# Moving the weight operations of a second MLP between the stages of a fused kernel

## The chip, the cores and the metric

The kernel runs on one core of one Trainium2 chip. The time is device microseconds from launch to end, the median of three runs. Five engines work beside each other, each through its own instructions in order: TensorE (PE in the profile, its weight loads PEld), VectorE (DVE), ScalarE (ACT), GpSimd (POOL) and SyncE (SP), which here issues nearly all DMA transfers. They wait for each other through semaphores.

## The reference

Attention without a softmax feeds two MLPs, all in float32:

```
kv  = einsum('bhsd,bhse->bhde', k, v)          # 8 batches, 8 heads, 576 rows, 64 columns
out = einsum('bhsd,bhde->bhse', q, kv)
x   = out / sqrt(mean(out*out, -1) + 1e-6) * g_norm      # then laid out as 4608 x 512
h   = x @ w_in                                 # 512 x 2048
y   = (s * max(h, 0)**2 + b) @ w_out           # 2048 x 512
z   = max(max(y @ w1, y @ w2), y @ w3)         # each 512 x 768
res = z @ w_out2                               # 768 x 512
```

## The kernel before, in words

A float32 product is made of three fast products. Each operand is split into a high part (ScalarE, a copy to the `float32r` type) and a low part (VectorE, the difference); high by high, low by high and high by low are summed in PSUM. The 4608 rows of x are nine tiles of 512. The weights come as 64-bit words and are converted on the core.

The stages, in order of time:

- **Opening and plain tiles** (tiles 0 and 1, first MLP): the start follows a list written out by hand (`OPENING`), the rest the loop over `slots` behind it. A slot is one block of 128 columns of h (there are 16, taken in groups of 3, 5 and 8): twelve up products `h`, the squared ReLU, its split (`gh`, `gl`: the gate), and twelve down products `y` two slots later. The last group of tile 1 is in this loop with `fa` = 8.
- **Tile 2** (`EDGE - 1`): the loop over `f` does the 16 up products and stores the squared ReLUs to `g_dr`, except for the last two blocks, which are gated directly. Then the pools of the plain stage close, and the class `Second` does the 16 down blocks: first the two direct ones, then blocks 0 to 13, whose squared ReLUs are loaded again as `gb` (`fetch`) and gated (`ready`).
- **Pairs 0, 1 and 2** (tiles 3 and 4, 5 and 6, 7 and 8): up products of two tiles at once by a seven-product scheme, by eight chunks `q` of two blocks each (products named `x`, `d`, `a`, `b`; ScalarE copies `a`, `p7`, `u2` between them), then a second half by `Second` for the second tile of the pair.
- **Second MLP**, from about 830 us on, with the same scheme for w1, w2, w3 and w_out2.

Attention for the tiles still to come runs beside all this in small steps (`rare_steps`): an item is `ops` (its products), `sq`, `og`, `sh`, `sl`, then `mps` (a mean by products with ones), `y`, `t` and the result `og`; `kvps` and `kvbd` make the matrix of a pair of heads.

The second MLP needs its weights combined for the seven-product scheme: nine operations `com_op(0)` to `com_op(8)` and three `out_op`. Each is made by `fused` (line 598 on): a load of two raw tiles, then for each of them `high` (ScalarE, L194) and `rest` (VectorE, L199 to L209), `sums` (VectorE, four differences, L696), `to_hi` (four copies on ScalarE, L639), `to_lo` (four on VectorE, L644) and six stores to `wc_dr`. Before, operations 0 and 1 stand beside tile 2's up products, 2 and 3 beside the second half of pair 0, 4 to 7 beside pair 1, and 8 in the second MLP.

What sets the order: `beside_of(fns, a, b)` spreads a list of steps evenly over a range of the clock `tick` counts (one tick for each TensorE product; `ONE` is 12). `store` puts a transfer off by some ticks, `dma` issues it at its place in the program. `tied_in` keeps a step behind the main work already written on ScalarE and VectorE (`in_order`). Within these ties a scheduler places each instruction on its engine when the program is built; what it decided is what `order` rows below show.

Memory: `rawp`, `wtp`, `wt1` and `stp` (raw tiles, two tables, staging tiles) belong to the plain stage; the pools of the pairs take the same memory when it closes. From then on the attention items share one PSUM bank (`ps_as`) where they had two.

Of the kernel before, what the change touches and what calls it, by code (L numbers as in the profile page):

```python
# [71 lines left out]
def fused_kernel(ctx, tc, qt, kv, kvr, g_norm, w_in, w_out, s, b, w1, w2, w3, w_out2, out):  # L72
# [525 lines left out]
    def fused(srcs, turned, target, dst, raws=None, tabs=wide, his=hi_tile):  # L598
# [42 lines left out]
        def to_lo(*ks):  # L641
            for k in ks:
                hi, lo, src = pieces()[k]
                nc.vector.tensor_tensor(out=lo, in0=src, in1=hi.bitcast(F32), op=ALU.subtract)  # L644

        def end():
            if target:
                if dst is not None:
                    store(dst, got["to"].bitcast(F32))
                return  # L650
            raw = blocks(got[0])
            to = [(0, 0, 2, got["to"].bitcast(F32)), (0, 2, 3, raw[:, 0:1]), (1, 0, 3, raw[:, 1:4]), (0, 3, 7, blocks(got[1]))]
            to += [(1, o, o + 2, blocks(t)) for o, t in zip((3, 5), got["tab"])]
            for z, a, e, t in to:
                store(dst[:, z, a:e], t, 12)

        def last():
            to_lo(*range(4))
            end()

        fns = [partial(high, 0), partial(rest, 0), none, partial(high, 1), partial(rest, 1), sums, none]
        if target:
            def both(k):
                to_hi(k + 1)
                to_lo(k)

            def close():
                to_lo(2)
                end()

            return load, fns + [partial(to_hi, 0), partial(both, 0), partial(both, 1), close]
        return load, fns + [partial(to_hi, *range(4)), last]

# [7 lines left out]

    def phased(op, before, behind):
        load, fns = op
        return [load] + [none] * before + [partial(tied_in, fn) for fn in fns] + [none] * behind

# [783 lines left out]
    pend = [(*slots[k], gates[k][1:]) for k in range(OPEN) if f"yy.{k}.0" not in ran]  # L1469

    todo, span, k_done, base = [], 1, 0, 0
    for i, sl in list(enumerate(slots))[OPEN:]:
# [10 lines left out]
        for half in range(2):  # L1483
            if half:
                if len(pend) == LAG:
                    u2(*pend.pop(0))
                pend.append((*sl, u1_end(h, n)))
            want = min(len(todo), -(-len(todo) * (2 * i + half + 1 - base) // span))
            while k_done < want:
                todo[k_done]()  # L1490
                k_done += 1


# [22 lines left out]

    def com_op(i, here=False, **homes):
        def target():
            wm[i] = wc_tile("wb" if i % 3 == 2 else "wa")
            return wm[i]  # L1520

        (ja, ma), (jb, mb) = sides_of(i)
        ws = w1, w2, w3
        return fused([chunk(ws[jb], mb), chunk(ws[ja], ma)], False, target if here else None, wc_dr[i], **homes)

    ONE = 3 * KD
# [4 lines left out]
    with in_order():  # L1531
        roots()
    beside_of(rare_steps(*groups[4]), 0, 24 * ONE)
    homes = {
        "raws": lambda: rawp.tile([P, 2 * DM], U32, tag="raw", name="raw"),
        "tabs": lambda: [p_.tile([P, DM], U32, tag=tg, name="tab") for p_, tg in ((wt1, "ta"), (wtp, "tb"))],
        "his": lambda: stage().bitcast(F32R).rearrange("p (n c) -> p n c", c=HW),
    }
    seq = []
    for i in range(2):  # L1540
        load, (h0, r0, _, h1, r1, sm, _, hi, lo) = com_op(i, **homes)
        seq += [load, none] if i == 0 else [none, load]
        seq += [lambda h0=h0, r0=r0: tied_in(h0, r0), lambda h1=h1, r1=r1: tied_in(h1, r1)]
        seq += [partial(tied_in, sm), partial(tied_in, hi), partial(tied_in, lo)]
    beside_of(seq, 2 * ONE, 16 * ONE)
    for f in range(KF):
        h = u1(t, 0, TW, f)
        if pend:
            u2(*pend.pop(0))
        r = wtp.tile([P, DM], U32, tag="tb", name="r").bitcast(F32) if f < 3 else stage()  # L1550
        squared(r, h)
        if f < KF - 2:
            store(g_dr[t][f], r)
        else:
            direct[f] = gate(r)
        tick(ONE)

# [256 lines left out]
    for s, (ta, tb) in enumerate(PAIRS):  # L1814
# [4 lines left out]
        if s == 1:  # L1819
            ops = [com_op(i) for i in range(4, NQ - 1)] + [out_op(KC - 1)]  # L1820
            beside_of([fn for op in ops for fn in phased(op, 4, 4)], 0, V + U - 12)
        if s == 2:
# [6 lines left out]
        for q in range(QF):  # L1829
            w = wcs.pop(q)  # L1830
            if s == 0 and 0 < q and q + 1 < QF:
                beside_of([prep.step], 3, 10)
            if s > 0 and 0 < q and q + 1 < QF:
                wcs[q + 1] = pair_load("wa", wp_dr[q + 1])
# [48 lines left out]
        beside_of(nxt, 10, 5 * QF * 6 - 8 if blk else U - 24)  # L1883
        if s == 0:
            beside_of([fn for i in (2, 3) for fn in phased(com_op(i), 3, 3)], 0, U - 12)
        if s + 1 < len(PAIRS):
# [24 lines left out]
    ops = [out_op(0, True), out_op(1, True), com_op(NQ - 1, True)]  # L1911
    inside += [fn for op in ops for fn in phased(op, 3, 1)]
    for si in range(len(SUPERS)):
# [100 lines left out]
```

## Time and profile before

| | |
|---|---|
| median of 3 runs | 1392.78 us (1390.97 to 1395.8) |
| profiled execution, its own time | 1389.79 us |
| span of the profile, first to last instruction | 1387.8 us |
| TensorE busy | 1361.1 us, 98% |
| VectorE busy | 994.7 us, 72% |
| ScalarE busy | 777.4 us, 56% |
| mean granted clock of TensorE | 0.996 |
| moved by DMA | 311.42 MB |

The time to read is the profiled execution's 1389.79, of which the span leaves 2 us outside. TensorE's busy time counts a product from its start to its modelled end, and neighbours overlap; a stretch where it is busy all the time can still be slow if its clock is low. A wait in square brackets at the end of a timeline row is the idle time of the engine ahead of that row, with the instruction that ended it.

### The profile page before, as it was taken

How to read it: one execution, taken by the hardware profiler on the slowest of the kernel's cores; microseconds unless marked ns; L12 is line 12 of the kernel's file. 1: busy time of each engine (PE TensorE's matmuls, PEld its weight loads, DVE VectorE, ACT ScalarE, POOL GpSimd, SP SyncE). 2: the span in 40 equal slices, each digit the busy share in tenths (PEclk: the TensorE clock that was granted, in tenths of full speed). 3: DMA queues.
4: the chain of work that ended last, by engine and by line, in shares of the span. 5: the costliest groups of instructions: out<-in, count | busy, mean ns of one | idle time of the engine just before them, and what ended most of it. 6: DMA issues, size and time to landing. Idle time of an engine off the chain costs nothing.

```text
span 1387.8 us, 19621 instructions
## 1 busy us (share of the span) xinstructions
PE 1361.1 (98%) x6822; PEld 1123.2 (81%) x6822; DVE 994.7 (72%) x1896; ACT 777.4 (56%) x1520; POOL 10.9 (1%) x40
## 2 busy tenths in 40 slices
PE   8999999989999999999999999999999999999998
PEld 6878787867888877888788878888998888888886
DVE  8998866868767578768667786797683675666555
ACT  7975655646777557667456775444453442444332
POOL 1000000000000000000000000000000000000000
PEclk9999999989999999999999999999999999999999
DMA  8486643778576686886847889656865554563432
GB/s 305 145 255 207 206 151 131 239 241 288 204 262 213 198 329 225 303 306 224 326 146 287 284 298 329 241 182 258 302 242 177 186 209 152 178 254 111 173 149 61
DMA packets 140457, 311.42 MB, mean 224 GB/s; under 512 B 50118, under 2 KB 71750, under 8 KB 131398
## 3 DMA queue, kind: packets, MB, share of 16 engines
q1 hardware_dynamic: 140352, 310.17, 64.2%
q8 instruction: 54, 0.88, 0.3%
q14 instruction: 45, 0.37, 0.1%
q10 hardware_dynamic: 6, 0.00, 0.0%
HBM read 218.89 MB, written 91.23 MB: 223 GB/s over the span
## 4 chain that ended last, share of the span: by engine, by line
PE 79%; DVE 10%; ACT 4%; DMA 4%; issue 2%; SPq 0%; DVEq 0%; ACTq 0%
PE x L520 19%; PE y L520 16%; PE d L520 12%; PE o L520 9%; PE b L520 6%; PE a L520 6%; PE h L445 3%; PE h L155 2%; PE y L155 2%; DVE tb L155 1%; PE ops L365 1%; DMA raw<-in_w_out 1%; DMA wq<-wo_dr 1%; PE kvps L343 1%; DMA wc<-ws_dr 1%
## 5 line engine op out<-in xcount | busy, mean ns | idle before, releaser
L520 PE MATMUL y<-gh,w 128*128 128x512 f32 x720 | 238.3, 394 | 2.2 <-ACT st L544 1.4
L520 PE MATMUL d<-t,wc 128*128 128x512 f32 (+1 forms) x828 | 200.0, 376 | 1.3 <-ACT p L810 1.3
L520 PE MATMUL x<-t,wc 128*128 128x512 f32 (+1 forms) x828 | 200.0, 376 | 0.0
L520 PEld LDWEIGHTS d<-t,wc 128*128 128x128 f32 x828 | 148.5, 188 | 29.5 <-ACT p L810 1.7
L520 PEld LDWEIGHTS x<-t,wc 128*128 128x128 f32 x828 | 148.4, 188 | 27.8 <-DVE t L181 0.2
L520 PEld LDWEIGHTS y<-gh,w 128*128 128x128 f32 x720 | 135.9, 189 | 30.6 <-ACT st L544 1.8
L520 PE MATMUL y<-gl,w 128*128 128x512 f32 x360 | 142.5, 396 | 1.7 <-DVE gl L503 1.6
L874 DVE TENSOR_TENSOR c<-d,u 128x512 f32<-128x512 f32 (+1 forms) x45 | 28.7, 638 | 115.6 <-PE d L520 115.5
L520 PE MATMUL a<-b,wc 128*128 128x512 f32 (+1 forms) x414 | 100.3, 376 | 0.0
L520 PE MATMUL x<-b,wc 128*128 128x512 f32 (+1 forms) x414 | 100.0, 376 | 0.0
L520 PE MATMUL b<-b,wc 128*128 128x512 f32 (+1 forms) x414 | 99.9, 377 | 0.0
L520 PEld LDWEIGHTS b<-b,wc 128*128 128x128 f32 x414 | 73.9, 188 | 15.3 <-ACT b L810 1.8
L520 PEld LDWEIGHTS x<-b,wc 128*128 128x128 f32 x414 | 74.3, 188 | 13.9 <-DVE c L878 0.2
L520 PEld LDWEIGHTS a<-b,wc 128*128 128x128 f32 x414 | 74.2, 188 | 13.9
L520 PEld LDWEIGHTS y<-gl,w 128*128 128x128 f32 x360 | 68.2, 189 | 17.1 <-DVE gl L503 4.1
L520 PE MATMUL o<-t,wq 128*128 128x512 f32 (+1 forms) x354 | 75.5, 369 | 0.0
L155 PE MATMUL h<-xh,w 128*128 128x512 f32 (+1 forms) x216 | 72.0, 377 | 0.7 <-ACT r L155 0.6
L869 ACT ACTIVATE a<-x 128x512 f32<-128x512 f32 (+1 forms) x45 | 24.3, 539 | 86.1 <-PE x L520 86.1
L520 PEld LDWEIGHTS o<-t,wq 128*128 128x128 f32 x354 | 62.4, 188 | 11.2
L503 DVE SCALAR_TENSOR_TENSOR gl<-r,cst,gh 128x512 fp32r<-128x512 f32 x56 | 42.0, 749 | 40.6 <-ACT gh L502 40.1
L869 ACT ACTIVATE b<-x 128x512 f32<-128x512 f32 (+1 forms) x45 | 24.3, 539 | 77.5 <-PE x L520 77.4
L155 PE MATMUL y<-gh,w 128*128 128x512 f32 (+1 forms) x200 | 65.3, 371 | 0.9 <-ACT st L155 0.9
(241 smaller groups left out, 2673.6 us busy)
## 6 DMA issues: line engine op xcount, KB each, us to landing
wc<-wc_dr SPq DMA_DIRECT2D x44, 1792.0 KB, 7.5
wc<-wp_dr SPq DMA_DIRECT2D x16, 1792.0 KB, 8.8
kv<-in_kv SPq DMA_DIRECT2D x32, 512.0 KB, 4.9
wp_dr<-wc SPq DMA_DIRECT2D x8, 1792.0 KB, 6.7
raw<-in_w_out SPq DMA_DIRECT2D x23, 512.0 KB, 5.0
gb<-g_dr SPq DMA_DIRECT2D x46, 256.0 KB, 5.5
g_dr<-r SPq DMA_DIRECT2D x43, 256.0 KB, 2.3
y_dr<-st SPq DMA_DIRECT2D x42, 256.0 KB, 3.0
```

Source lines behind the costliest of these rows:

```text
L155: tail[eng] = call(*args, **kw).ins
L343: nc.tensor.matmul(pb[d, i * D:(i + 1) * D], lhsT=t[:, 0, d], rhs=t[:, 1, d], start=(c == 0), stop=(c == NC))
L365: nc.tensor.matmul(pb, lhsT=l, rhs=r, start=(i == 0), stop=(i == 2))
L445: nc.tensor.matmul(h[:, :n], lhsT=w[:, z, kk, :], rhs=x[:, kk, o:o + n], start=(i == 0), stop=(i == 3 * KD - 1))
L503: nc.vector.scalar_tensor_tensor(out=gl, in0=r, scalar=b, in1=gh.bitcast(F32), op0=ALU.add, op1=ALU.subtract).ins,
L520: ins = nc.tensor.matmul(*args, **kw)
L869: main["act"] = nc.scalar.activation(out=out, in_=pb, func=ACTF.Copy).ins
L874: main["dve"] = nc.vector.tensor_tensor(out=o, in0=pb, in1=t, op=ALU.add).ins
```

## The change

`fused` issues its stores at their place (`dma`) and returns one plain list of steps, the stores being a step of their own; `phased` takes a string that says, for each step of the spread, what is done: `L` load, `h` and `r` the two conversion steps, `s` the sums, `a` and `b` the high and low parts, `e` the stores, a dot nothing. Operation 0 goes into the last group of tile 1, one step each half slot. Operations 1 and 2 go beside tile 2 from its first tick over 150 ticks (before: operations 0 and 1 from tick 24 to 192), with the clock counted in two halves of a block. Operation 3 begins in chunk 7 of pair 0 and runs 153 ticks on, into that pair's second half, where 2 and 3 were. Both tables of the early operations now come from `wt1`. The strings for pair 1 and the second MLP keep the same steps with the stores as a step behind.

```diff
--- before.py
+++ after.py
@@ -646,30 +646,24 @@
         def end():
             if target:
                 if dst is not None:
-                    store(dst, got["to"].bitcast(F32))
+                    dma(out=dst, in_=got["to"].bitcast(F32))
                 return
             raw = blocks(got[0])
             to = [(0, 0, 2, got["to"].bitcast(F32)), (0, 2, 3, raw[:, 0:1]), (1, 0, 3, raw[:, 1:4]), (0, 3, 7, blocks(got[1]))]
             to += [(1, o, o + 2, blocks(t)) for o, t in zip((3, 5), got["tab"])]
             for z, a, e, t in to:
-                store(dst[:, z, a:e], t, 12)
-
-        def last():
-            to_lo(*range(4))
-            end()
-
-        fns = [partial(high, 0), partial(rest, 0), none, partial(high, 1), partial(rest, 1), sums, none]
+                dma(out=dst[:, z, a:e], in_=t)
+
+        fns = [partial(high, 0), partial(rest, 0), partial(high, 1), partial(rest, 1), sums]
         if target:
             def both(k):
                 to_hi(k + 1)
                 to_lo(k)
 
-            def close():
-                to_lo(2)
-                end()
-
-            return load, fns + [partial(to_hi, 0), partial(both, 0), partial(both, 1), close]
-        return load, fns + [partial(to_hi, *range(4)), last]
+            fns += [partial(to_hi, 0), partial(both, 0), partial(both, 1), partial(to_lo, 2), end]
+        else:
+            fns += [partial(to_hi, *range(4)), partial(to_lo, *range(4)), end]
+        return load, fns
 
     def tied_in(*fns):
         with in_order():
@@ -679,9 +673,10 @@
     def none():
         pass
 
-    def phased(op, before, behind):
+    def phased(op, order):
         load, fns = op
-        return [load] + [none] * before + [partial(tied_in, fn) for fn in fns] + [none] * behind
+        fns = [partial(tied_in, fn) for fn in fns]
+        return [load if c == "L" else none if c == "." else fns.pop(0) for c in order]
 
     def sides_of(i):
 
@@ -1468,6 +1463,21 @@
     OPEN = next(k for k in range(len(slots)) if f"up.{k}.0" not in ran)
     pend = [(*slots[k], gates[k][1:]) for k in range(OPEN) if f"yy.{k}.0" not in ran]
 
+    def com_op(i, here=False, **homes):
+        def target():
+            wm[i] = wc_tile("wb" if i % 3 == 2 else "wa")
+            return wm[i]
+
+        (ja, ma), (jb, mb) = sides_of(i)
+        ws = w1, w2, w3
+        return fused([chunk(ws[jb], mb), chunk(ws[ja], ma)], False, target if here else None, wc_dr[i], **homes)
+
+    homes = {
+        "raws": lambda: rawp.tile([P, 2 * DM], U32, tag="raw", name="raw"),
+        "tabs": lambda: [wt1.tile([P, DM], U32, tag="ta", name="tab") for _ in range(2)],
+        "his": lambda: stage().bitcast(F32R).rearrange("p (n c) -> p n c", c=HW),
+    }
+    early = phased(com_op(0, **homes), "L.h.r.h.rs.a.b.e")
     todo, span, k_done, base = [], 1, 0, 0
     for i, sl in list(enumerate(slots))[OPEN:]:
         t, o, n, f, fa, fb = sl
@@ -1489,6 +1499,8 @@
             while k_done < want:
                 todo[k_done]()
                 k_done += 1
+            if early and fa == BLOCKS[-1][0] and t == EDGE - 2:
+                early.pop(0)()
 
 
     sides = []
@@ -1514,15 +1526,6 @@
         sides.clear()
         stores_due(math.inf)
 
-    def com_op(i, here=False, **homes):
-        def target():
-            wm[i] = wc_tile("wb" if i % 3 == 2 else "wa")
-            return wm[i]
-
-        (ja, ma), (jb, mb) = sides_of(i)
-        ws = w1, w2, w3
-        return fused([chunk(ws[jb], mb), chunk(ws[ja], ma)], False, target if here else None, wc_dr[i], **homes)
-
     ONE = 3 * KD
     clock[0] = 0
     flush_held()
@@ -1531,20 +1534,11 @@
     with in_order():
         roots()
     beside_of(rare_steps(*groups[4]), 0, 24 * ONE)
-    homes = {
-        "raws": lambda: rawp.tile([P, 2 * DM], U32, tag="raw", name="raw"),
-        "tabs": lambda: [p_.tile([P, DM], U32, tag=tg, name="tab") for p_, tg in ((wt1, "ta"), (wtp, "tb"))],
-        "his": lambda: stage().bitcast(F32R).rearrange("p (n c) -> p n c", c=HW),
-    }
-    seq = []
-    for i in range(2):
-        load, (h0, r0, _, h1, r1, sm, _, hi, lo) = com_op(i, **homes)
-        seq += [load, none] if i == 0 else [none, load]
-        seq += [lambda h0=h0, r0=r0: tied_in(h0, r0), lambda h1=h1, r1=r1: tied_in(h1, r1)]
-        seq += [partial(tied_in, sm), partial(tied_in, hi), partial(tied_in, lo)]
-    beside_of(seq, 2 * ONE, 16 * ONE)
+    seq = [fn for i in (1, 2) for fn in phased(com_op(i, **homes), "L..hrhrs.ab.e..")]
+    beside_of(seq, 0, 5 * len(seq))
     for f in range(KF):
         h = u1(t, 0, TW, f)
+        tick(ONE // 2)
         if pend:
             u2(*pend.pop(0))
         r = wtp.tile([P, DM], U32, tag="tb", name="r").bitcast(F32) if f < 3 else stage()
@@ -1553,7 +1547,7 @@
             store(g_dr[t][f], r)
         else:
             direct[f] = gate(r)
-        tick(ONE)
+        tick(ONE - ONE // 2)
 
     stores_due(math.inf)
     plain.close()
@@ -1818,7 +1812,7 @@
             beside_of(rare_steps(*groups[5 + s]), 0, V + U - 10)
         if s == 1:
             ops = [com_op(i) for i in range(4, NQ - 1)] + [out_op(KC - 1)]
-            beside_of([fn for op in ops for fn in phased(op, 4, 4)], 0, V + U - 12)
+            beside_of([fn for op in ops for fn in phased(op, "L....hr.hrs.ab..e...")], 0, V + U - 12)
         if s == 2:
             attn.close()
             w2p["cp"] = pool("cp", 1, st=mlp1)
@@ -1830,6 +1824,8 @@
             w = wcs.pop(q)
             if s == 0 and 0 < q and q + 1 < QF:
                 beside_of([prep.step], 3, 10)
+            elif s == 0 and q:
+                beside_of(phased(com_op(3), "L....hr.hrs.ab..e"), 20, 20 + 17 * 9)
             if s > 0 and 0 < q and q + 1 < QF:
                 wcs[q + 1] = pair_load("wa", wp_dr[q + 1])
             fill, end = [], q == QF - 1
@@ -1881,8 +1877,6 @@
             del yt[ta, 0]
         nxt = x_of(s + 1) if s + 1 < len(PAIRS) else y_of(0)
         beside_of(nxt, 10, 5 * QF * 6 - 8 if blk else U - 24)
-        if s == 0:
-            beside_of([fn for i in (2, 3) for fn in phased(com_op(i), 3, 3)], 0, U - 12)
         if s + 1 < len(PAIRS):
             for i, at in ((0, 45), (1, 100)):
                 beside_of([lambda i=i: wcs.update({i: pair_load("wa", wp_dr[i])})], at, at + 1)
@@ -1909,7 +1903,7 @@
     for i in range(3):
         wm_load(i)
     ops = [out_op(0, True), out_op(1, True), com_op(NQ - 1, True)]
-    inside += [fn for op in ops for fn in phased(op, 3, 1)]
+    inside += [fn for op in ops for fn in phased(op, "L...hr.hrs.aaabe")]
     for si in range(len(SUPERS)):
         nxt = y_of(si + 1) if si + 1 < len(SUPERS) else []
         small = SUPERS[si][1] < TW
```

On SyncE, where tile 2 goes from up products to down products (`gb` are the squared ReLUs loaded again, `wc_dr` the stores of a weight operation, `F` a pair's raw weights, `kv` attention, `x_dr` its results). Before:

```order
L161 DMA kv_3385<-in_kv 128x1024
L161 DMA kv_3385<-in_kvr 64x256
L177 DMA wc_dr1_245<-st_3321 128x512
L177 DMA wc_dr1_245<-raw_3158 128x256
L177 DMA wc_dr1_245<-raw_3160 128x1024
L177 DMA x_dr4_127<-og_3314 128x256
L177 DMA wc_dr1_245<-raw_3158 128x768
L177 DMA wc_dr1_245<-tab_3201 128x512
L177 DMA wc_dr1_245<-tab_3202 128x512
L161 DMA gb_3429<-g_dr2_0_132 128x512
L161 DMA gb_3431<-g_dr2_1_133 128x512
```

Now:

```order
L161 DMA qt_3478<-in_qt 128x256
L161 DMA F_3676<-wi_dr1_197 128x512
L161 DMA F_3676<-wi_dr0_196 128x512
L161 DMA F_3679<-wi_dr3_199 128x512
L161 DMA kv_3428<-in_kv 128x1024
L161 DMA kv_3428<-in_kvr 64x256
L161 DMA kv_3432<-in_kv 128x1024
L161 DMA kv_3432<-in_kvr 64x256
L177 DMA x_dr4_127<-og_3366 128x256
L161 DMA gb_3466<-g_dr2_0_132 128x512
L161 DMA gb_3468<-g_dr2_1_133 128x512
```

The stores of the second operation no longer stand ahead of `gb`; three `F` loads do, and the `kv` loads stand there as before.

On ScalarE, beside tile 2's up blocks 10 to 12 (`st<-h` is the ReLU of a block: before, `st_3147`, `st_3175`, `st_3222` are blocks 10, 11 and 12, now `st_3217`, `st_3251`, `st_3290`). Before:

```order
L460 ACTIVATE st_3147<-h_3134 128x512
L405 ACTIVATE y0_3127<-mps_3124,cst_115 128x256
L406 ACTIVATE t_3128<-y0_3127 128x256
L460 ACTIVATE st_3175<-h_3162 128x512
L367 ACTIVATE sq_3183<-ops_3179 128x256
L368 ACTIVATE og_3184<-ops_3179,cst_115 128x256
L180 ACTIVATE sh_3187<-sq_3183 128x256
L180 ACTIVATE qh_3227<-qt_3082 128x256
L405 ACTIVATE y0_3194<-mps_3191,cst_115 128x256
L406 ACTIVATE t_3195<-y0_3194 128x256
L460 ACTIVATE st_3222<-h_3209 128x512
```

Now:

```order
L180 ACTIVATE sh_3247<-sq_3243 128x256
L180 ACTIVATE qh_3284<-qt_3132 128x256
L639 ACTIVATE st_3212<-raw_3067 128x512
L460 ACTIVATE st_3217<-h_3192 128x512
L639 ACTIVATE raw_3067<-raw_3067 128x256
L460 ACTIVATE st_3251<-h_3225 128x512
L639 ACTIVATE raw_3069<-tab_3101 128x512
L639 ACTIVATE raw_3069<-tab_3102 128x512
L405 ACTIVATE y0_3257<-mps_3254,cst_115 128x256
L406 ACTIVATE t_3258<-y0_3257 128x256
L460 ACTIVATE st_3290<-h_3270 128x512
```

The weight operation's `tab` and its copies (L639) now stand between these ReLUs, one copy ahead of that of block 10.

On TensorE, from the last down block of pair 0 to the first of pair 1 (`w31` is the weight of the last block, `w2` of the first; `wc` the pair's first weights). Before:

```order
L520 MATMUL y3_5490<-gh_5833,w31_2086 128x512
L520 MATMUL d_5911<-t3_5767,wc_5569 128x512 x2
L520 MATMUL x_5898<-t2_5801,wc_5569 128x512 x3
L520 MATMUL y0_5466<-gl_5834,w31_2086 128x512
L520 MATMUL y0_5466<-gh_5833,w31_2086 128x512
L520 MATMUL y1_5477<-gl_5834,w31_2086 128x512
L520 MATMUL y1_5477<-gh_5833,w31_2086 128x512
L520 MATMUL y2_5486<-gl_5834,w31_2086 128x512
L520 MATMUL y2_5486<-gh_5833,w31_2086 128x512
L520 MATMUL y3_5490<-gl_5834,w31_2086 128x512
L520 MATMUL y3_5490<-gh_5833,w31_2086 128x512
L520 MATMUL d_5911<-t4_5703,wc_5569 128x512 x3
```

Now:

```order
L520 MATMUL y3_5534<-gh_5844,w31_2086 128x512
L520 MATMUL y3_5534<-gl_5845,w31_2086 128x512
L520 MATMUL y3_5534<-gh_5844,w31_2086 128x512
L520 MATMUL d_5912<-t3_5634,wc_5620 128x512 x3
L520 MATMUL d_5912<-t3_5793,wc_5620 128x512 x3
L520 MATMUL x_5899<-t2_5666,wc_5620 128x512 x3
L520 MATMUL x_5899<-t2_5821,wc_5620 128x512 x3
L520 MATMUL a_5906<-b21_5689,wc_5620 128x512 x3
L520 MATMUL a_5906<-b21_5834,wc_5620 128x512 x3
L520 MATMUL d_5912<-t4_5736,wc_5620 128x512 x3
L520 MATMUL d_5912<-t4_5854,wc_5620 128x512 x3
L520 MATMUL x_5899<-t1_5752,wc_5620 128x512 x3
```

The last down block no longer has `d` and `x` in its middle, and `a` stands between the two parts of `x` and `d`.

## Rows read from the trace of the kernel before

**Rows 1.** The page's first part: busy us (share of the span) and instructions of each engine.
```profile
PE 1361.1 (98%) x6822; PEld 1123.2 (81%) x6822; DVE 994.7 (72%) x1896; ACT 777.4 (56%) x1520; POOL 10.9 (1%) x40
```

**Rows 2.** Stretches: length, each engine's busy us (instructions), granted clock, DMA share, GB/s.
```profile
166.00:216.00 50.00, 50.00 (x297) 41.34 (x296) 36.23 (x74) 30.35 (x74) 1.23 (x4) 1.00 0.42 135
216.00:281.00 65.00, 64.57 (x395) 52.32 (x394) 50.00 (x111) 38.40 (x91) 1.64 (x6) 1.00 0.58 194
281.00:303.00 22.00, 16.70 (x61) 12.03 (x61) 12.60 (x28) 10.12 (x24) 0.20 (x1) 0.77 0.84 278
...
500.00:538.00 38.00, 35.48 (x152) 27.54 (x152) 30.77 (x56) 21.00 (x38) 0.00 (x0) 1.00 0.67 251
...
290.60:301.00 10.40, 7.79 (x23) 5.27 (x23) 4.56 (x10) 4.20 (x9) 0.00 (x0) 0.51 0.90 275
```

**Rows 3.** Timeline of TensorE, 278 to 303: start, us, line, operation, shapes, count, [wait].
```profile
278.15 0.39 PE L445 MATMUL h<-xh,w 128*128 128x512 f32 x1
...
280.71 0.50 PE L520 MATMUL y<-gh,w 128*128 128x512 f32 x1
...
286.07 0.39 PE L520 MATMUL y<-gh,w 128*128 128x512 f32 x1
...
288.08 0.38 PE L402 MATMUL mps<-sh,ones 128*128 128x256 f32 x1 [1.14 <-ACT sh L180]
...
290.39 0.40 PE L365 MATMUL ops<-qh,kvbd 128*128 128x256 f32 x1 [1.47 <-DVE t L407]
...
295.28 2.08 PE L520 MATMUL y<-gh,w 128*128 128x512 f32 x4
...
301.55 0.62 PE L520 MATMUL y<-gh,w 128*128 128x512 f32 x2
...
302.25 0.62 PE L520 MATMUL y<-gh,w 128*128 128x512 f32 x2
```

**Rows 4.** Timeline of SyncE's DMA queue, 281 to 291.
```profile
281.81 0.54 SPq L177 DMA_DIRECT2D wc_dr<-st  x1
...
287.66 0.95 SPq L177 DMA_DIRECT2D wc_dr<-tab  x2
288.65 1.83 SPq L161 DMA_DIRECT2D gb<-g_dr  x2
```

**Rows 5.** The tile `gb`, 250 to 330: its 14 loads from issue to landing.
```profile
DMA to landing us min/median/max: 4.0/5.2/5.9
```

**Rows 6.** Timeline of ScalarE and VectorE, 288 to 295.
```profile
288.96 0.47 ACT L405 ACTIVATE y<-mps,cst 128x256 f32<-128x256 f32 x1 [0.63 <-PE mps L403]
289.46 0.42 ACT L406 ACTIVATE t<-y 128x256 f32<-128x256 f32 x1
...
294.26 1.32 ACT L502 ACTIVATE gh<-gb,cst 128x512 fp32r<-128x512 f32 x2
...
289.91 0.42 DVE L407 SCALAR_TENSOR_TENSOR t<-mps,t 128x256 f32<-128x256 f32 x1 [1.10 <-ACT t L406]
```

**Rows 7.** The tile `tab` in the stretch of both operations: length, VectorE and ScalarE busy.
```profile
239.00:288.00 49.00, 16.30 (x32) 5.19 (x8) 1.00 0.67 225
```

**Rows 8.** Timelines of TensorE and of ScalarE, 499 to 537.
```profile
499.25 0.50 PE L520 MATMUL y<-gl,w 128*128 128x512 f32 x1 [0.39 <-DVE gl L503]
...
531.00 0.40 PE L520 MATMUL y<-gh,w 128*128 128x512 f32 x1
532.66 1.66 PE L520 MATMUL d<-t,wc 128*128 128x512 f32 x6 [1.26 <-ACT p L810]
...
536.53 0.73 PE L520 MATMUL y<-gh,w 128*128 128x512 f32 x2 [0.84 <-ACT gh L502]
...
530.51 0.69 ACT L544 ACTIVATE st<-y,cst 128x512 f32<-128x512 f32 x1 [0.30 <-PE y L520]
...
532.02 0.59 ACT L810 ACTIVATE p<-d 128x512 f32<-128x512 f32 x1
```

## The prediction

> **What bounds the kernel now.** I read the page first: TensorE is busy 98% of the span, VectorE 72%, ScalarE 56% [rows 1]. The edits touch no matrix product, so the time can only move where TensorE waits or runs at its lower clock. The busy time by stretch is the next view [rows 2]: beside tile 1's last block (166 to 216 us) TensorE loses nothing, beside tile 2's up products (216 to 281) 0.4 us; from 281 to 303 it is busy 16.70 of 22 us, and from 500 to 538 35.48 of 38. The timeline of TensorE shows what happens from 286 on [rows 3]: the last up product ends at 278.5, the two direct blocks of tile 2's second half at 286.5; then come four waits of 1.14 and 1.47 us (each twice, the first of each is shown) inside one chain of attention items through a single PSUM bank, and the down products of block 0 start only at 295.28. Their operand is `gb`, and SyncE's timeline says why it is late [rows 4]: its load is issued at 288.65, directly behind the last stores of the second weight operation (`wc_dr`). It lands 4.0 to 5.9 us later [rows 5], and the gate starts at 294.26 [rows 6]. Behind this hole the granted clock is 0.51, the 1.2 GHz level, from 290.6 to 301 [rows 2]. The other place is the turn from pair 0 to pair 1 [rows 8].
>
> **The change part by part.**
>
> *Removed: the second operation's tail before tile 2's second half (term A).* Let E be that end of the last up product, 278.5 now. Before, block 0 starts at E + 16.8. In the new order six `wc_dr` stores stand no longer between `kv` and `gb`; operation 2 ends around up block 11. What stands ahead of `gb` instead: three `F` loads, four `kv` loads that wait for the attention products at about E + 2.2, and one `x_dr` store, whose item is finished on VectorE at about E + 3.1. With the issues themselves `gb` goes out at about E + 4 and lands by the median at E + 9.2 (8.0 to 9.9) [rows 5]. TensorE meanwhile has 40 small products (2.2 us, until 280.71 [rows 3]), the 24 direct down products at 0.23 us each, from three in 0.70 [rows 3], and two items; I count E + 8.0 when they are out except the last `ops`. That waits for the item before it, from the end of its `mps`: 0.47 + 0.42 + 0.42 plus hand-overs, 1.4 as the row 290.39 shows [rows 3, 6], so it starts at E + 9.0; `sq` (0.4) stands on ScalarE ahead of the gate (0.7 of the 1.32 for two) [rows 6], and block 0 starts at E + 10.3. That is 6.5 us sooner. Before, the hole also did one more item and six small products (0.8 us), which must now be done elsewhere: 5.7. From 295.28 to 300.9 the products ran at half the clock, 5.6 us of which half would not be needed: 2.6 with the first waits. Term A is -8.3. Bounds: -10.9 if the whole hole goes (22.0 minus 16.70, and the half clock), -2 if `gb` lands at E + 13 and the clock still falls.
>
> The Trainium skill (DMA: Bandwidth & Descriptors, section Anatomy of one DMA) says that the wait for a semaphore sits with the sequencer that issues the transfer, so nothing passes it; the 288.65 agrees. By that rule `gb` waits for `kv` in the new order and term A is as above; if it could pass, it would land near E + 6 and term A would be about -9.5.
>
> *Added: a whole operation beside tile 1's last block (term D).* One operation's instructions on its two tables take 16.30 / 2 = 8.2 us of VectorE and 2.6 of ScalarE [rows 7], with the pieces that touch only `raw` some 9 and 3.6. The 50 us there have 36.23 of VectorE busy, so 45 of 50: it fits. A block's gate is due two blocks after its up product, 12 us later (8 blocks in the 50 us), and its own chain is four instructions, so an overfull block (by the new order and these durations the second gets 8.3 us of VectorE work in 7.3) is absorbed. Price between 0 and 2.2 us (the operation's sums and a conversion half in one block); I take 0.5, near the 50.00 that TensorE keeps at 72% VectorE.
>
> *Moved: two operations packed beside tile 2 (term C).* They begin with the tile rather than 24 ticks in and end by up block 11. The first fits: counted in the same way, blocks 2 to 5 carry 15 us of VectorE work in 17 of TensorE. The second is crowded into one place, shown for ScalarE in the new order. From the end of up block 9: the squared ReLU is out at 1.2 us; ten instructions of the operation at 0.51 (16.30 / 32 [rows 7]) and five of attention at 0.42 [rows 6] end at 8.4; then `st<-raw` and, behind it, the ReLU of block 10, 0.65 each (5.19 / 8 [rows 7]): 9.7. Block 12 needs that ReLU to free its bank, two banks serving in turn. TensorE has two up products (24 at 0.23) and two items, 6.7 us. It waits up to 3.0; neighbouring instructions overlap, so 2.6. The 0.4 lost there before goes: +2.2, between 0 and +5 (the full 8.3 of VectorE work against one block's 3.2).
>
> *Moved: operations out of pair 0's second half (term B).* Two stood there, now the end of one. TensorE's new order finishes all down products and then runs `d`, `x`, `a`, `d`, so that six or twelve products (1.4 or 2.8 us) cover each copy on ScalarE. Before, `d` was split around the last down products, and its second half waited 1.26 us for the copy `p`, which stood behind the two scalings `st<-y` [rows 8]; then block 0 of pair 1 waited 0.84 for its gate. Together 2.4 with the slow restarts; new waits of up to 0.5 (four instructions of 0.7, 2.8 us, from `a` to the gate's second part, against twelve products and an `mps` pair, 3.0): -2.0, between -4 and +1.
>
> *The rest.* The queue edits (`dma` in place of a delayed `store`, half ticks, one step more per operation) add no instruction. In pairs 1 and 2 TensorE's order differs in a few places, and from 658 us on not at all: 0, plus or minus 1. The second MLP's last operation stores one step later, hidden behind loads that use it a pass later.
>
> Sum: -8.3 + 0.5 + 2.2 - 2.0 = -7.6 against the profiled run's 1389.8 (span 1387.8): 1382.2. The median of the runs shown is 1392.8, 3.0 above that run, and the same 3.0 goes on the forecast: 1385.2.
>
> **The rivals.**
>
> *The hole stays half open.* `gb` needs the eighth transfer before it to be finished (the order lists such a wait on nearly every transfer), and that is now `F`, 0.25 MB. With 0.84 of the DMA time taken in that stretch [rows 2] loads stretch, `gb` lands at E + 13, and block 0 starts at E + 14. Then 2.8 - 0.8 = 2.0 is won, terms B, C, D leave +0.7: -1.3, 1391.5. Against it: the `wc_dr` stores, 1.8 MB by the size of their tile, are gone from exactly this stretch. Here the clock falls as before. The Trainium skill (TensorE: Matmul & The Clock Gate, section HAM oscillation) says a matmul engine that idles long enough between bursts returns at half rate; the 0.51 agrees, and the 1.00 of 500 to 538 with waits of 1.3 and 0.8 us does too. By that rule term A keeps its 2.6 if the waits are as short as I count; otherwise it is -5.7.
>
> *More is won than I count.* Term C does not appear (the loads come early enough that the ten instructions spread out), A is whole, and the two waits of 0.39 on `gl` in pair 0's half (one is shown [rows 8]) go with the slow start behind each, 1.1: -10.9 - 2.4 - 1.1 + 0.5 = -13.9, 1378.9.
>
> *VectorE becomes the bound beside tile 2.* This one ends slower. Both crowded places (the tails of operations 1 and 2) then hold TensorE for their full excess, 2.9 and 5.2 us, and each time the clock falls to the lower level for about 10 us as at 290.6, half of it lost: 8.1 + 2 x 5.0 = 18.1, less 10.3 of A and B and plus 0.5: +8.3, 1401. With one fall it is +3.3, 1396. For it speaks that VectorE's work over 166 to 281 rises from 86 to 95 us; against it that this is still 83% of the stretch. It decides from the point where the two waits exceed 10 us together with the clock.
>
> *The moves do nothing* because the order is a scheduler's: excluded, since the order of the built program shows them.
>
> **How the numbers follow.** Forecast 62%, its own range 1381 to 1388.5; half open 14%; more won 14%; VectorE bound 10%. About 0.3% (4.2 us) is what a measurement of this kernel can tell from no change. Faster by more: 0.62 x 0.98 + 0.14 and a little of the half-open case, 0.77; slower by more: most of the fourth, 0.07; within: 0.16. The range leaves out the deep end of the second rival and the fourth: 1380 to 1392.
>
> **What would show it.** Right: in the new profile `gb<-g_dr` is issued within 6 us of the last up product, no stretch near 285 to 300 has a clock below 1.00, and the `d<-p` wait is gone. Term C right: TensorE waits about 2 us for ScalarE's ReLU of block 10 in tile 2. Wrong: a clock below 1.00 anywhere before that point, `gl` or `sl` waits over 1 us in tile 1's last block, or new waits in pair 0 from the operation beside its last up chunk.

## The result, and the profile after

The changed kernel takes 1380.18 us (median of 4 runs, 1379.77 to 1380.87) against 1391.88 us for the kernel before beside it: 0.9912, 95% interval 0.9891 to 0.9933, or -11.7 us. Two later comparisons gave 0.9927 (0.9915 to 0.9939) and 0.9905 (0.9892 to 0.9918). The forecast was -7.6 us, or 1385.2 us with its own range of 1381 to 1388.5: the direction and the places were right, the gain was too small by 2 to 5 us, and the time lies below the range. Of the 5.0 us between 1385.2 and 1380.18, 4.1 are the gain; the other 0.9 come from the base, a median of 1392.78 for the kernel before where the runs with the change beside it gave 1391.88.

To see where it came from, the same TensorE instruction is looked up in the timeline of before and in that of the changed kernel; the difference of the two starts, followed along the run, grows or shrinks where time is lost or won. The table has its increase by stretch (times on the clock of before), for three profiles of the changed kernel: the first, k9_change_again and k11_change_beside. A figure holds to about 0.1 us.

| Stretch, us (before) | Term | Predicted | First | k9 | k11 |
|---|---|---|---|---|---|
| 0 to 163 | none, the order is the same | 0 | +2.8 | +4.1 | +2.7 |
| 163 to 212 | D, tile 1's last group | +0.5 | +0.2 | +0.4 | +0.4 |
| 212 to 278 | C, tile 2's up products | +2.2 | +2.2 | +3.7 | +2.3 |
| 278 to 309 | A, the hole | -8.3 | -8.7 | -8.7 | -8.7 |
| 309 to 350 | A, the rest of that half | 0 | -1.2 | -1.6 | -0.6 |
| 350 to 545 | B, pair 0 and the turn | -2.0 | -4.2 | -4.6 | -4.1 |
| 545 to the end | rest | 0 | -1.2 | -0.5 | +0.1 |
| sum | | -7.6 | -10.1 | -7.3 | -7.8 |

The first line is no term of the change. Every engine's instructions stand in the same order in both kernels up to there, yet in the profiles of this study that stretch took from 0.6 us less to 5.7 us more than in the profile of before; in that one the opening was among the shortest. The lines of D, C, A and B sum to -11.7, -10.8 and -10.6 us; the timed comparisons lie around that (-11.7, and by their ratios about -10 and -13).

The page's first line, and the stretches that answer to [rows 2]:

```profile
PE 1356.7 (98%) x6822; PEld 1121.6 (81%) x6822; DVE 993.1 (72%) x1896; ACT 776.1 (56%) x1520; POOL 11.0 (1%) x40
```
```profile
169.00:219.00 50.00, 50.00 (x296) 40.98 (x294) 42.31 (x91) 33.04 (x80) 1.40 (x4) 1.00 0.50 167
219.00:286.00 67.00, 65.38 (x396) 52.93 (x396) 54.17 (x121) 41.07 (x97) 1.83 (x6) 1.00 0.72 245
286.10:299.60 13.50, 11.64 (x55) 9.33 (x54) 7.27 (x16) 6.47 (x16) 0.00 (x0) 1.00 0.81 277
495.20:529.20 34.00, 33.95 (x151) 27.62 (x150) 20.34 (x32) 17.87 (x33) 0.00 (x0) 1.00 0.58 218
```

Tile 1's last group of blocks takes 42.31 us of VectorE instead of 36.23 and TensorE loses nothing. Beside tile 2 it now loses 1.6 us. The stretch of 22 us that had TensorE busy for 16.70 takes 13.5 us with 11.64 busy, all at 1.00. Before the turn to pair 1 it is busy 33.95 of 34. TensorE's timeline at the end of tile 2's up block 9, at the two waits of tile 2 and at the former hole:

```profile
261.78 0.39 PE L445 MATMUL h<-xh,w 128*128 128x512 f32 x1
...
268.13 0.39 PE L445 MATMUL h<-xh,w 128*128 128x512 f32 x1
268.36 0.28 PE L365 MATMUL ops<-qh,kvbd 128*128 128x256 f32 x1
...
268.59 0.28 PE L365 MATMUL ops<-qh,kvbd 128*128 128x256 f32 x1
270.02 0.38 PE L402 MATMUL mps<-sh,ones 128*128 128x256 f32 x1 [1.14 <-ACT sh L180]
270.32 0.39 PE L365 MATMUL ops<-qh,kvbd 128*128 128x256 f32 x1
270.64 0.38 PE L403 MATMUL mps<-sl,ones 128*128 128x256 f32 x1
271.45 0.50 PE L445 MATMUL h<-xh,w 128*128 128x512 f32 x1 [0.43 <-ACT st L460]
...
283.30 0.39 PE L445 MATMUL h<-xh,w 128*128 128x512 f32 x1
...
292.66 0.39 PE L365 MATMUL ops<-qh,kvbd 128*128 128x256 f32 x1 [0.78 <-DVE t L407]
...
294.37 1.19 PE L520 MATMUL y<-gh,w 128*128 128x512 f32 x4 [1.08 <-ACT gh L502]
```

E, the end of the last up product, is 283.7; block 0 starts at E + 10.7 (before: E + 16.8; forecast: E + 10.3). SyncE's queue, and the landing of the 14 `gb` loads:

```profile
287.29 0.41 SPq L177 DMA_DIRECT2D x_dr<-og  x1
287.74 1.97 SPq L161 DMA_DIRECT2D gb<-g_dr  x4
```
```profile
DMA to landing us min/median/max: 3.4/5.4/5.7
```

`gb` goes out at E + 4.0, as counted, against E + 10.1 in [rows 4]. ScalarE at the second wait of tile 2:

```profile
270.28 0.63 ACT L639 ACTIVATE st<-raw 128x512 fp32r<-128x512 f32 x1
270.82 0.58 ACT L460 ACTIVATE st<-h 128x512 f32<-128x512 f32 x1
```

The ReLU of block 10 (L460) stands behind `st<-raw` (L639), as forecast. The two waits are parts of one stall, and this ReLU ends it: the last `ops` is over at 268.87, the ReLU at 271.40, and the up products of block 12 start at 271.45. Inside that time TensorE's order has two `mps` and one `ops` of the attention items, the first of them after 1.14 us for its `sh`. The 0.43 in the row of block 12 is only the end of the stall.

### The profile page after: what moved, and what is told of

Read it like the earlier page. It is cut to its first block, busy times and chain, and to the rows that moved or that the text cites. A ratio compares the mean times of both kernels' runs of the same rounds, so it can differ in the third digit from the quotient of the medians.

```text
span 1377.8 us, 19620 instructions
## 1 busy us (share of the span) xinstructions
PE 1356.7 (98%) x6822; PEld 1121.6 (81%) x6822; DVE 993.1 (72%) x1896; ACT 776.1 (56%) x1520; POOL 11.0 (1%) x40
## 4 chain that ended last, share of the span: by engine, by line
PE 82%; DVE 8%; DMA 5%; ACT 3%; issue 2%; SPq 0%; DVEq 0%; ACTq 0%
PE x L520 19%; PE y L520 15%; PE d L520 13%; PE o L520 9%; PE b L520 7%; PE a L520 6%; PE h L445 5%; PE y L155 2%; PE h L155 2%; PE ops L365 1%; DVE tb L155 1%; PE kvps L343 1%; DMA wq<-wo_dr 1%; DVE head L155 1%; DMA raw<-in_w_out 1%
## 5 line engine op out<-in xcount | busy, mean ns | idle before, releaser
L520 PEld LDWEIGHTS y<-gl,w 128*128 128x128 f32 x360 | 67.7, 188 | 13.5 <-DVE gl L503 1.0
```

Of the source, the lines that this page charges most:

```text
L520: ins = nc.tensor.matmul(*args, **kw)
```

## The experiments

Theory: each place has its own price, and the gain is the hole (A) and the turn (B) less the crowd in tile 2 (C). The main rivals: one common effect of the new steps and queue edits; the stores in SyncE's queue alone; the opening. In what follows "by 350 us" and the like are the increases read as in the table.

**k1_one_op_tile2: A without C and B.**
```
-    seq = [fn for i in (1, 2) for fn in phased(com_op(i, **homes), ...)]
-    beside_of(seq, 0, 5 * len(seq))
+    seq = phased(com_op(1, **homes), "L..hrhrs.ab.e..")
+    beside_of(seq, 0, 9 * len(seq))
...
-            elif s == 0 and q:
-                beside_of(phased(com_op(3), "L....hr.hrs.ab..e"), 20, 20 + 17 * 9)
...
+        if s == 0:
+            beside_of([... (2, 3) ... phased(com_op(i), "L...hr.hrs.abe...")], 0, U - 12)
```


> Operation 0 beside tile 1's last block and operation 1 alone (spread over 11 blocks) beside tile 2, as in the change less operation 2; operations 2 and 3 both in pair 0's second half, as before the change. Theory (each place has its own price: hole -9, crowding in tile 2 +2.3, turn to pair 1 -4): the hole goes (gb issued within 5 us of the last up product, no half clock at 285 to 303), no wait of 1 us for ScalarE's ReLU in tile 2, the waits for p, gh and gl at the turn stay; -9 us against the kernel before, ratio 0.9935. Rival (the gain is one effect, of the queue edits or the finer steps): as fast as the change, 0.991, and the waits at the turn are gone. Second rival (the hole went because operation 2 ended early, not because less work stands there): the waits of 290 come back, under -4 us.

0.994 (0.9927 to 0.9954). The hole: -10.2 from 278 to 350. Tile 2: +0.4 in place of +2.2. The turn: +1.0, worse than before, with one wait of 2.31 us there, and the granted clock at half behind it:

```profile
497.53 0.50 PE L520 MATMUL y<-gl,w 128*128 128x512 f32 x1 [2.31 <-DVE gl L503]
```
```profile
498.00:501.40 3.40, 3.40 (x10) 2.62 (x9) 3.40 (x7) 1.75 (x4) 0.00 (x0) 0.50 0.72 286
```

So the terms come apart as the theory says, and one common effect is excluded. VectorE is busy all of these 3.40 us, which fits two operations beside pair 0's second half as what the turn pays for; k2 tests it.

**k2_turn_alone: B alone, on the kernel before.**
```
-        if s == 0:
-            beside_of([fn for i in (2, 3) for fn in phased(com_op(i), 3, 3)], 0, U - 12)
+            elif s == 0 and q:
+                beside_of(phased(com_op(3), 4, 3), 20, 20 + 17 * 9)
...
-            ops = [com_op(i) for i in range(4, NQ - 1)] + ...
+            ops = [com_op(i) for i in (2, *range(4, NQ - 1))] + ...
```


> The kernel before with pair 0's second half relieved alone: operation 3 beside the last up chunk of pair 0 as in the change, operation 2 in pair 1 as the first of its operations; operations 0 and 1 and tile 2 as before. Theory: hole and half clock at 286 to 301 as before; the four waits at the turn (d for p 1.26, y for gh 0.84, two for gl 0.8) and the slow restart behind each gone, -4.0 us by 540 us; ratio 0.997. Rival (the waits at the turn come from how late pair 0's second half starts or from the new steps): they stay, 1.000. Third: operation 2 costs what it cost in pair 1 instead, new waits between 540 and 800 us, 1.000 or above.

1.0037 (1.0024 to 1.005): slower. The turn did what the theory said, -4.0 us from 350 to 545, with no wait left; the hole stayed (+1.2), and its four long waits with it. But operation 2 in pair 1 cost 9.7 us by 713, more than it saved: the third case.

```profile
502.90:536.90 34.00, 34.00 (x150) 27.26 (x149) 20.02 (x32) 17.75 (x31) 0.00 (x0) 1.00 0.59 218
...
665.60:672.50 6.90, 4.20 (x10) 3.21 (x11) 6.40 (x14) 3.61 (x7) 0.00 (x0) 0.51 0.62 224
```
```profile
668.30 0.79 PE L520 MATMUL y<-gh,w 128*128 128x512 f32 x1 [4.62 <-DVE st L546]
```

**k3_stores_other_queue: the six stores alone, on the kernel before.**
```
+                if raws and dst is wc_dr[1]:
+                    nc.gpsimd.dma_start(out=dst[:, z, a:e], in_=t)
+                else:
                     store(dst[:, z, a:e], t, 12)
```


> The kernel before with the six wc_dr stores of operation 1 issued on GpSimd's queue, nothing else moved. Tells the stores in SyncE's queue from VectorE's tail of the operation, both of which stood before gb. Theory (both share it): gb now stands behind the x_dr store alone, which waited for og until E + 7.4 (285.9), so gb goes out at E + 7.8 instead of E + 10.2: -2.4 us, and the clock still falls behind the hole; ratio 0.998. Rival (the stores are all of it): gb by E + 5, hole and half clock gone, -8, 0.994. Second rival (the stores did nothing): 1.000.

1.0001 (0.9992 to 1.0011). From 278 to 309 it wins 2.6 us, loses 1.0 again by 350 at a wait for `gl` (2.07) and 1.1 at another at 501. E is 281.2, so the rows show `gb` at E + 8.6 behind a store that waits for `og`, which VectorE finishes late, and block 0 at E + 15.0:

```profile
289.47 0.33 SPq L177 DMA_DIRECT2D x_dr<-og  x1
289.84 2.11 SPq L161 DMA_DIRECT2D gb<-g_dr  x4
```
```profile
291.64 0.39 PE L402 MATMUL mps<-sh,ones 128*128 128x256 f32 x1 [1.14 <-ACT sh L180]
...
293.96 0.58 PE L365 MATMUL ops<-qh,kvbd 128*128 128x256 f32 x1 [1.47 <-DVE t L407]
...
296.22 2.07 PE L520 MATMUL y<-gh,w 128*128 128x512 f32 x4 [1.25 <-ACT gh L502]
```

So the stores in SyncE's queue account for 2.6 us of the 8.7 at the hole, as the theory had it, and by itself the edit gains nothing. The rest the theory puts down to the operation's tail on VectorE, where this `og` stands behind the operation's instructions; no run took that tail away alone.

**k4_op2_in_pair1: the change without C.**
```
+    seq = phased(com_op(1, **homes), "L..hrhrs.ab.e..")
+    beside_of(seq, 0, 9 * len(seq))
...
+            ops = [com_op(i) for i in (2, *range(4, NQ - 1))] + [out_op(KC - 1)]
```


> The changed kernel with operation 2 taken from beside tile 2 and put in pair 1 as the first of its operations; operation 1 alone spread over 11 blocks of tile 2. Theory: the two waits in tile 2 for ScalarE's ReLU of block 10 and what hangs on it (1.3 and 0.7 us in the changed kernel's trace) go and pair 1 hides the operation: -2.3 us against the changed kernel, 0.9895 of the kernel before. Rival (the two waits come from the tile's own chain, not from the operation): as the change, 0.991. Third: pair 1 pays for it with waits of its own, 0.991 or above, waits between 540 and 800 us.

0.9959 (0.9946 to 0.9971). C is gone (-0.3 from 212 to 278), A is -10.6, B -3.9; then pair 1 pays 7.9 us:

```profile
651.95 0.50 PE L520 MATMUL y<-gh,w 128*128 128x512 f32 x1 [2.17 <-ACT st L544]
654.61 0.79 PE L520 MATMUL y<-gh,w 128*128 128x512 f32 x1 [2.16 <-DVE st L546]
```
```profile
653.60:660.40 6.80, 5.79 (x14) 4.53 (x15) 2.68 (x5) 0.69 (x1) 0.00 (x0) 0.50 0.96 327
```

The waits in tile 2 go with operation 2, and pair 1 has no room for a sixth operation.

**k5_spread_steps: C by spreading.**
```
-    ... phased(com_op(i, **homes), "L..hrhrs.ab.e..")]
+    ... phased(com_op(i, **homes), "L..h.rh.rs.ab.e..")]
```


> The changed kernel with the steps of operations 1 and 2 beside tile 2 spread: an empty step between the absolute value and the rest of each half, 18 steps of 5 ticks in place of 16, so that the ten VectorE instructions of operation 2 stand in six steps rather than four and its end moves from block 12 to block 14. Theory (the waits of 1.14 and 0.43 us in tile 2 come from this crowding): they go or halve, gb still goes out at E + 4 (E is the end of the last up product): -1 to -2 us against the change, 0.990 of the kernel before. Rival: the crowd only moves towards the end, the waits stay, and the tail delays gb again: 0.992 to 0.994, gb later than E + 6.

0.9939 (0.9926 to 0.9952). Read at the last up product, tile 2 costs +0.8 in place of +2.2 to +3.7, but A falls to -6.6: `gb` goes out at 285.72, E + 5.6, and there is a wait of 1.51 for `gh` with 3.4 us at half clock behind it. Mostly the rival: an operation that ends later takes the gain back.

```profile
279.69 0.40 PE L445 MATMUL h<-xh,w 128*128 128x512 f32 x1
...
291.36 1.45 PE L520 MATMUL y<-gh,w 128*128 128x512 f32 x4 [1.51 <-ACT gh L502]
```

**k6_outop_in_last_pair and k8_outop_earlier: a place for the sixth operation.**
```
k6 (on k4):
-            ops = [com_op(i) for i in (2, *range(4, NQ - 1))] + [out_op(KC - 1)]
+            ops = [com_op(i) for i in (2, *range(4, NQ - 1))]
+        if s + 1 == len(PAIRS):
+            beside_of(phased(out_op(KC - 1), "L....h.r.h.r.s.a.b.e"), 0, 150)
k8: the same operation at (34, 34 + 100) in the last pair's last up chunk
```


> k4_op2_in_pair1 with as many operations in pair 1 as the change has there: the operation on the output weights that stood last in pair 1 is moved to the last pair's second half, where VectorE is busy 73%. Theory (k4 lost its 7.9 us at the turn from pair 1 to pair 2 because five operations and one stood there, one more than fit): the waits of 2.2 and 2.2 us and the half clock at 650 go, tile 2 and the turn to pair 1 stay as in k4, so -2.2 us against the change: 0.9895 of the kernel before. Rival: the place is at fault, not the number (operation 2 first in the row delays the others): loss at 650 stays, 0.996. Third: the last pair pays instead, waits over 2 us between 740 and 815, 0.992 or above.

> k6_outop_in_last_pair with the operation on the output weights begun earlier: at the end of the last pair's last up chunk, over 100 ticks, so that its six wo_dr stores leave SyncE's queue before the loads b<-g_dr of that half start. Theory (k6 lost 3.8 us at 851 because those stores, waiting for VectorE, stood in SyncE's queue ahead of the b loads, as wc_dr did ahead of gb): the waits of b for gh and gl there go, the rest stays as in k6; -3 us against the change, 0.989 of the kernel before. Rival (any operation in the last pair holds its blocks): new waits between 780 and 850 in place of those, as k6, 0.9935.

0.9936 (0.9922 to 0.9949) and 0.9953 (0.9935 to 0.997). With the sixth operation out of pair 1, the loss at 650 is gone (0 in both), so it was the number. But the last pair pays: in k6 3.8 us at 851, where `wo_dr` stores stand among the loads of `b`; in k8 5.2 us at 826, where a load of `wc` comes 3.27 late. In its queue:

```profile
802.54 0.37 SPq L161 DMA_DIRECT2D wc<-ws_dr  x1
808.27 0.32 SPq L161 DMA_DIRECT2D wo_dr<-hi  x1
...
810.25 2.50 SPq L161 DMA_DIRECT2D wo_dr<-raw  x3
812.80 1.89 SPq L161 DMA_DIRECT2D wo_dr<-tab  x2
814.78 0.83 SPq L161 DMA_DIRECT2D wc<-ws_dr  x1
...
823.27 0.37 SPq L161 DMA_DIRECT2D wc<-ws_dr  x1
```
```profile
826.50 0.77 PE L520 MATMUL x<-gh,wc 128*128 128x512 f32 x1 [3.27 <-DMA wc<-ws_dr]
```

That the stores are what makes this `wc` late is likely from the order of the queue, not shown by a run of its own.

**k7_earlier_end_alone: only an earlier end, on the kernel before.**
```
-    beside_of(seq, 2 * ONE, 16 * ONE)
+    beside_of(seq, 0, 13 * ONE)
```


> The kernel before with one edit: operations 0 and 1 beside tile 2 begin with the tile and end after 13 blocks instead of running from block 2 to block 16. No operation beside tile 1, operations 2 and 3 in pair 0's second half. Theory (the hole comes from the operation's tail at the end of tile 2, on VectorE and in SyncE's queue, not from how many stand there): hole and half clock go, -9.8, the crowding costs some +2 in tile 2, the waits at the turn to pair 1 stay: -7 to -8 us, 0.9945. Rival (it takes the operation beside tile 1 to close the hole): gb later than E + 7, half clock again, 0.998 or above.

0.9966 (0.9955 to 0.9976), between the theory and its rival. One line wins a good part of the hole. E is 278.1, so `gb` goes out at E + 6.7 (before: E + 10.1) and block 0 starts at E + 12.6 (before: E + 16.8); that is -5.4 from 278 to 350. Tile 2 costs +0.3, the turn +0.6. From 212 to 350 it makes -5.0, where the first profile of the change has -7.7. The gain is smaller than expected because two waits still follow each other before block 0, with 3.4 us at half clock behind them, and a wait for `gl` of 1.18 comes at 327:

```profile
284.46 0.33 SPq L177 DMA_DIRECT2D x_dr<-og  x1
284.85 0.96 SPq L161 DMA_DIRECT2D gb<-g_dr  x2
```
```profile
277.74 0.39 PE L445 MATMUL h<-xh,w 128*128 128x512 f32 x1
...
288.83 0.39 PE L365 MATMUL ops<-qh,kvbd 128*128 128x256 f32 x1 [0.78 <-DVE t L407]
...
290.68 1.57 PE L520 MATMUL y<-gh,w 128*128 128x512 f32 x4 [1.24 <-ACT gh L502]
```

So more than half of what the hole gives back comes without the operation beside tile 1. What that operation buys besides is the place that B empties.

**k9_change_again and k11_change_beside: the change, twice more.** No edit.

> The changed kernel once more, unaltered, beside the other on the same chip. Theory (of the 10.0 us between the two profiled spans, +2.8 in the opening and -1.3 at 825 are not the change's: a load of wc that landed late, and the clock at the start): the stretch up to 160 us differs from the first profile of it, the stretches from 163 to 820 repeat within 0.3 us: +2.2 in tile 2, -9.8 at the hole, -4.2 at the turn; no wait for wc at 825. Rival (the opening belongs to the change): +2.8 by 160 us again. Ratio 0.9912.

> The changed kernel unaltered, beside k10, to compare the two on one chip. Theory: tile 2 costs 2.2 us, or 3.7 where the clock falls behind its waits, the hole gives 9.8 to 10.2 back, the turn 4.2 to 4.6; ratio to the kernel before between 0.991 and 0.993. Rival (the terms change from chip to chip): any of them off by more than 1 us.

The terms are in the table: A at the hole repeats to 0.1 us and B to 0.5; C is 2.3 or, with the clock falling behind its waits in k9, 3.7. The opening was not settled by k9: it gave +4.1, not less. Three things bear on it. The order up to 163 us is that of before. k10, with the same operation beside tile 1, has +1.8, k5 +0.5 and k6 +0.2. And k3, the kernel before but for the stores at 282, has +2.4. So it varies from run to run; why is open but for the part told in the last section. No profile but the one of before has the wait of 1.05 us for `wc` near 825 with its order there unchanged, so this -1.3 was a late landing in that one execution.

**k10_op2_spread_same_end: C by spreading, with the end kept.**
```
+    ... ((1, "L..hrhrs.ab.e."), (2, "L..h.rh.rs.ab.e..")) for fn in phased(com_op(i, **homes), s)]
```


> The changed kernel with operation 2's steps beside tile 2 spread as in k5, but begun three steps earlier (the empty steps behind operation 1 are dropped), so that it ends where it ends in the change. Theory (C is the crowd of operation 2's ten VectorE and four ScalarE instructions, which lets TensorE's order place mps straight behind ops; the hole depends on where the operation ends): the waits of 1.14 and 0.43 us in tile 2 fall below 0.5 together and the clock stays up there, gb goes out by E + 4.5, the loss at the hole as in the change: -1.5 to -3 us against the change run beside it. Rival (an operation spread into block 10 to 12 costs at the hole what it saves before, as k5 did): no change against it, a half clock behind the last up product.

0.9904 (0.9889 to 0.9919), 1379.29 us against 1380.13 for the change beside it: too close for these runs to tell apart. The traces can: from 212 to 278 it loses nothing (-0.1 against +2.3), TensorE is busy all of the stretch below, and A is -9.1 against -9.3. Together that is 2.3 us won, by a shift of empty steps. `gb` was expected by E + 4.5 and went out at E + 5.7; block 0 starts at E + 10.3 even so.

```profile
250.00:281.00 31.00, 31.00 (x145) 24.84 (x143) 26.95 (x59) 21.18 (x50) 0.00 (x0) 1.00 0.83 297
```

## Why the prediction was right or wrong

**Term A, -8.3, right at the hole and short behind it.** Measured -8.7 in all three profiles from 278 to 309. Its steps hold one by one: `gb` out at E + 4.0 (E + 4), landing in 5.4 us (5.2), the last `ops` at 292.66, E + 9.0 (E + 9.0), block 0 at E + 10.7 (E + 10.3), no half clock. The size is in part luck: counted from E, block 0 starts 6.1 us sooner and not 6.5, and with the 2.6 behind it that makes the 8.7; the 0.8 taken off for products to be done elsewhere was too much. What the term lacked is the 0.6 to 1.6 us from 309 to 350. The kernel before has a wait for `gl` at 333.39 that the sum did not hold, since the view of the stretch ended at 303:

```profile
333.39 0.50 PE L520 MATMUL y<-gl,w 128*128 128x512 f32 x1 [0.86 <-DVE gl L503]
```

In the three profiles of the change it is gone; k5 (0.92) and k7 (1.18) still have it although most of their hole is gone. There, as before, `gl` stands on VectorE behind the pieces for pair 0's weights (`wc<-G`, 1.2 us); in the change it stands ahead of them. Why the order differs wasn't tried.

**Term B, -2.0, the term that was mis-sized.** Measured -4.2, -4.6 and -4.1, and -4.0 alone in k2. The mechanism was right: the two long waits [rows 8] are gone. Three steps of the sum failed. With the slow products behind them these waits were worth 3.3 us in all three profiles (2.9 in k2) rather than 2.4. The new waits of up to 0.5 did not come. And the two waits of 0.39 for `gl`, which I left to a rival, went in k2 too, so they belong to the same cause: 0.9, 1.4 and 0.9 us with what follows them, 1.1 in k2. The rival had the piece that was missing, at 1.1. Together with A's end this is the gap of 3 to 4 us between the table's lines of D, C, A and B and the -7.6.

**Term C, +2.2, right in size and in cause.** +2.2, +2.3 and, with the clock falling, +3.7. The forecast had TensorE out of other work 6.7 us after the end of up block 9 and the ReLU of block 10 done at 9.7; in the first profile, from 262.17 on, they are 6.7 (the last `ops`) and 9.2 (the ReLU). Three small products run in these 2.6 us, which elsewhere take 0.12 each (the rows from 268.36 to 268.59), so about 2.2 are lost. That one of them shows a wait for `sh` was not forecast; the up products could not have started sooner without it, since they need the ReLU. k1, k4, k6 and k8 (no operation 2 there) and k10 (spread) show that the stall comes from the crowd.

**Term D, +0.5.** +0.2 to +0.4. Kernels with no operation beside tile 1 show +0.3 (k2, k3) and -0.2 (k7) in the same stretch, so it is about nothing.

**The rest, 0.** Held from 545 us on to 1.5 us or better, but for the load at 825 that came late in the profile of before. k9 and k11 have a wait of 0.7 to 0.8 for `wc<-wc_dr` near 985 that the first profile and the one of before have not; k7, which stores as before, has one of 0.41.

**The rivals.** The half open hole: excluded, `gb` went out at E + 4.0 and landed by the median 5.4 us later, not at E + 13. VectorE as the bound beside tile 2: its mechanism is real but came as 2.2 to 3.7, not 8.1 and two falls of the clock. "More is won" had the two `gl` waits right and C wrong, and its A of -10.9 was about as near to the measured -9.3 to -10.3 as the -8.3 was. That is luck: -10.9 is the 5.3 us idle and all of the 5.6 us at half clock, of which the prediction itself gives only half back.

## What to carry to other kernels

In this kernel most of what work beside a stage cost was paid where it ended: its tail on VectorE delayed the small operations, and its stores the loads, that open the next stage. End it some blocks before the turn (k7: one line, 5 us of the 7.7 there), and spread it so that its own crowd doesn't come in one block (k10). When the price of a turn is summed up, count every wait on the engine that is relieved, not only the longest, and read on past the end of the hole.

## What the runs showed of the hardware

The same waits were followed by a fall of the granted clock in one execution and not in another. The waits of 1.14 and 0.43 us in tile 2 stand in all three profiles of the change; in k9 alone TensorE then ran at half clock (the 1.2 GHz level), which made C 1.4 us dearer (the stretch in k9):

```profile
273.20:276.50 3.30, 3.30 (x9) 2.58 (x8) 3.30 (x7) 2.25 (x5) 0.00 (x0) 0.50 0.82 315
```

Waits of 0.78 and 1.08 before block 0 brought no fall in any of the three; 0.78 and 1.24 did in k7, as did 0.78 and 1.51 in k5, for 3.4 us. And at the start of the program the three profiles of the change have such a fall, at 10.0 to 10.4 us, which before does not have (10 us from 7 us on, first profile of the change and before):

```profile
7.00:17.00 10.00, 8.97 (x81) 6.11 (x78) 6.80 (x17) 6.28 (x15) 0.00 (x0) 0.83 1.04 397
```
```profile
7.00:17.00 10.00, 9.90 (x109) 7.20 (x108) 8.87 (x23) 8.16 (x21) 0.00 (x0) 1.00 1.04 386
```

It is not the change's: k3, with the order of before, has it at 9.3, while k5 and k6, with the change's order up to there, have none. The fall lasts 3.4 us, so it can explain 1.7 of the first profile's 2.8 in the opening; k6 has +0.9 by 15 us without one.
